# Squares on ScalarE and low-part products last, while float64 weights are converted in a chained attention, MoE and feed-forward kernel

## The chip, the cores and the metric

The kernel runs on one core of one Trainium2 chip. The metric is the device time of one execution in microseconds, as the median of several runs. Five engines of the core work side by side, each through its own list of instructions in order: TensorE (matmul), VectorE, ScalarE, GpSimd, and SyncE, which here starts DMA transfers.

## The reference

A sliding-window attention with sink tokens feeds a top-1 mixture of experts, and that feeds a second, dense feed-forward. The change lies in the last part:

```python
def _moe2_ref(x, w_in, w_out):          # x 1536x512, w_in 512x2048, w_out 2048x512
    h = x @ w_in
    r = np.maximum(h, 0.0)
    g = r * r
    return (g @ w_out).astype(np.float32)
```

The weights w_in and w_out arrive as float64; everything else is float32.

## The kernel before

**Precision.** A float32 operand is split into a high part of type float32r and a low part, the rest. A product of two split operands is then three matmuls: high x high, high x low, low x high. The names end in h and l: gh and gl for the activations, wh and wl (yh and yl, or xh and xl, as tiles) for the weights.

**The converter.** The two float64 weight matrices are read as pairs of 32-bit integers, in 16 pieces of 1 MB, eight of w_in and eight of w_out, and rebuilt as float32 by `piece_stage` (L174 to L189). A piece passes four stages. Stage 0: ScalarE scales the upper words (L180), VectorE shifts the lower words (L181). Stage 1: VectorE joins them in two operations (L183, L184). Stage 2: ScalarE writes the high part (L186). Stage 3: VectorE writes the low part (L188), and the raw tile is free for the transfer of a later piece; there are three such tiles of 1 MB. One call of `tick` (class `Ticks`, L191) finishes the piece that is open and begins the next: old stage 2, new stage 0, old stage 3, new stage 1, in that order on each engine. The list of pieces alternates between w_out and w_in after the first two. Three ticks run within the last expert; `ticks.close()` finishes the open piece, and 13 pieces remain. `ticks.done()` is true once the list is used up and nothing is open.

**The second feed-forward.** The 1536 tokens go in three chunks of 512 (index c), the 2048 hidden features in 16 blocks of 128 (index f), so there are 48 steps (c, f). `run` goes through them by the order written out there:

```python
            stage_a(c, f)      # 12 matmuls: block f of h, transposed, 128 x 512 tokens
            stage_g(c, f)      # ScalarE gh, VectorE gl
            tick()             # one round of the converter, while there is work
            if turn:
                its.pop(0)()   # transposes for the next chunk, at f = 7, 9, 11, 13
            if prev:
                stage_b(*prev) # 12 matmuls of the step before: 4 row blocks x 3 products
            prev = c, f
```

`stage_a` ends with the Relu on ScalarE (L1112, from PSUM to an SBUF tile called xb in the trace) and the square on VectorE (L1113, in place). `stage_g` makes gh from it on ScalarE (L1128) and gl on VectorE (L1130). `stage_b` (L1169) adds g @ w_out for one feature block into four PSUM tiles, one for each block of 128 tokens, and works through them one after the other, each with its three products. TensorE's order is thus a(f), b(f-1), a(f+1), b(f), and so on. With 13 pieces left, tick has work in the first 14 steps (c = 0, f = 0 to 13), and `ticks.done()` is still false when `stage_a` runs in each of these 14. When `stage_b` runs, after the tick, it is false for the blocks f = 0 to 11. A piece of w_out serves two feature blocks.

Of the kernel before, what the change touches and what calls it, by code (L numbers as in the profile page):

```python
# [12 lines left out]
AF = mybir.ActivationFunctionType  # L13
# [3 lines left out]
P = 128  # L17
# [15 lines left out]
def kernel(  # L33
# [15 lines left out]
    nc = tc.nc  # L49
# [8 lines left out]
    NFF = FF // P  # L58
# [27 lines left out]
    def ps(tag, name):  # L86
        banks[tag].append(banks[tag].pop(0))
        return psum.tile([P, 512], F32, tag=f"b{banks[tag][-1]}", name=name)
# [10 lines left out]
    def raw_tile(n=1):  # L99

        nonlocal slot
        slot += slot % n
        t = RAW[slot // 2 % len(RAW)][:, slot % 2 * 1024 : slot % 2 * 1024 + n * 1024]
        slot += n
        return t
# [657 lines left out]
    for u in range(len(units) + PL + 1):  # L763
# [4 lines left out]
        if u < len(units):  # L768
            n, c = units[u]
# [17 lines left out]
        m, c = divmod(u, HP)  # L787
# [196 lines left out]
    ticks = Ticks(order)  # L984
# [17 lines left out]
    def load_y(c, tags):  # L1002

        c0, w = chunks[c]

        def ld(t):
            if t < w // P:
                r0 = c0 + t * P
                nc.sync.dma_start(yts[t % len(yts)], yd[r0 : r0 + P, :])

        def go(t):
            yt = yts[t % len(yts)]
            p_ = ps(tags[t % 2], "x2T")
            for kk in range(KD):
                nc.tensor.transpose(p_[:, kk * P : (kk + 1) * P], yt[:, kk * P : (kk + 1) * P], ident)  # L1015
            n = c0 // P + t
            nc.gpsimd.tensor_copy(tok[:, n : n + 1], yt.bitcast(I32)[:, DM:])
            pv = p_.rearrange("p (k n) -> p k n", k=KD)
            hv, lv = (x[:, :, t * P : (t + 1) * P] for x in x2T[c])
            nc.scalar.copy(hv, pv)  # L1020
            nc.vector.tensor_sub(lv, pv, hv.bitcast(F32))  # L1021
            ld(t + len(yts))

        for t in range(len(yts)):
            ld(t)
        return [lambda t=t: go(t) for t in range(w // P)]
# [70 lines left out]
    outp, gT, its, scattered = {}, {}, [], []  # L1097

    def stage_a(c, f):
        nonlocal its  # L1100
        if f == 0:
            its = load_y(c + 1, ("pt", "ot")) if c + 1 < NCH else []
        a_ = ps("bg", "a")
        xh, xl = x2T[c]
        w = width[c]
        for kk in range(KD):
            r = slice(f % 2 * 512 + kk * P, f % 2 * 512 + kk * P + P)
            wh, wl = WI.h[f // 2][:, r], WI.l[f // 2][:, r]
            for m, (a, bb) in enumerate(((wh, xh), (wh, xl), (wl, xh))):
                nc.tensor.matmul(a_[:, :w], a, bb[:, kk, :w], start=(kk == 0 and m == 0), stop=(kk == KD - 1 and m == 2))  # L1110
        r_ = xring[f % 2, last][:, :w]
        nc.scalar.activation(r_, a_[:, :w], AF.Relu)  # L1112
        nc.vector.tensor_mul(r_, r_, r_)  # L1113
        gT[c, f] = r_


# [4 lines left out]
    def packed(c):  # L1121
        return width[c] % P if 0 < width[c] % P <= 64 else 0
# [12 lines left out]
    def scatter(n, o_, rows):  # L1135
        i = nc.gpsimd.indirect_dma_start(  # L1136
            out=out, out_offset=bass.IndirectOffsetOnAxis(ap=tok[:rows, n : n + 1], axis=0), in_=o_[:rows, :], in_offset=None,
            bounds_check=NTOK - 1, oob_is_err=False,
        )

        for x in scattered:
            tc.declare_no_dep(i.ins, x.ins, reason="rows of different tokens")
        scattered.append(i)

    def blocks(c):

        ts = list(range((width[c] + P - 1) // P))
        return ts[-1:] + ts[:-1] if packed(c) else ts

    def stage_b(c, f, only=None):  # L1150
        gh, gl = gT[c, f]
        w, k_ = width[c], packed(c)
        nt = (w + P - 1) // P
        if f == 0:
            outp[c] = [ps("s" if t < 3 else "iv", "out") for t in range(nt)]
        wh, wl = WO.h[f // 2], WO.l[f // 2]
        r = slice((f % 2) * 512, (f % 2) * 512 + 512)
        for t in blocks(c) if only is None else [only]:
            cs = slice(t * P, min(w, (t + 1) * P))
            rows = cs.stop - cs.start  # L1160
            o = outp[c][t]
            if k_ and t == nt - 1:
                prods = ((gh[:, cs.start : w + k_], wh), (gh[:, cs.start : w + k_], wl))
                o = o[: 2 * k_, :]
            else:
                prods = ((gh[:, cs], wh), (gh[:, cs], wl), (gl[:, cs], wh))
                o = o[:rows, :]
            for m, (a, bb) in enumerate(prods):
                nc.tensor.matmul(o, a, bb[:, r], start=(f == 0 and m == 0), stop=(f == NFF - 1 and m == len(prods) - 1))  # L1169
            if f == NFF - 1:  # L1170
                n = chunks[c][0] // P + t
                o_ = raw_tile()[:, :DM]
                if k_ and t == nt - 1:
                    nc.scalar.copy(o_[:k_, :], o[k_ :, :])
                    nc.vector.tensor_add(o_[:k_, :], o_[:k_, :], o[:k_, :])
                elif t % 2:
                    nc.scalar.copy(o_[:rows, :], o)
                else:
                    nc.vector.tensor_copy(o_[:rows, :], o)
                scatter(n, o_, rows)  # L1180
# [5 lines left out]
    def run(steps, prev):  # L1186

        for c, f in steps:
            turn = f >= 7 and f % 2 and its
            stage_a(c, f)  # L1190
            stage_g(c, f)
            tick()
            if turn:
                its.pop(0)()
            if prev:
                stage_b(*prev)
            prev = c, f
        return prev

    def end(c, prev):  # L1200

        nonlocal slot
        slot = 0
        for f in (NFF - 2, NFF - 1):
            stage_a(c, f)
            stage_g(c, f)
        stage_b(*prev)
        for t in blocks(c):
            stage_b(c, NFF - 2, t)
            stage_b(c, NFF - 1, t)  # L1210
# [60 lines left out]
```

## Time and profile before

| | us |
|---|---|
| median of 3 runs | 607.14 |
| lowest and highest of them | 607.09, 607.84 |
| the profiled execution, its own time | 608.54 |
| span of the profiled execution | 606.8 |
| TensorE busy (share of span) | 575.8 (95%) |
| VectorE busy | 354.9 (58%) |
| ScalarE busy | 297.2 (49%) |
| GpSimd busy | 136.5 (22%) |

The span goes from the first to the last instruction; the profiled execution's own time is longer than that by 1.7 us. Rows of the trace are all from this one execution. Busy shares are averages over parts of the kernel that have different limits. A matmul's shown duration overlaps with the next one's, since they are pipelined: the pace is the distance between starts.

### The profile page before, as it was taken

To read this page: it belongs to the slowest core of one execution; us is meant where nothing else is said; L and a number is where in the kernel's file an instruction comes from. 1 tells how busy PE (TensorE), PEld (TensorE's weight loads), DVE (VectorE), ACT (ScalarE), POOL (GpSimd) and SP (SyncE) were. 2 spreads that over 40 slices of the span, in tenths; PEclk is the share of its full clock that TensorE was granted. 3 is DMA by queue.
4 is the path that set the end of the run, shared out by engine and by line. 5 is a ranking of instruction groups with operands and counts; after the bars stand their busy time and mean duration, and the time that the engine had idled before them with its cause. 6 is when DMAs were issued, how large, how long until landed. Compare 5 with 4: busy or idle time off the path is not lost. (4 is left out here: it accounts for less than half of the span.)

```text
span 606.8 us, 9356 instructions
## 1 busy us (share of the span) xinstructions
PE 575.8 (95%) x3243; PEld 458.7 (76%) x3243; DVE 354.9 (58%) x838; ACT 297.2 (49%) x649; POOL 136.5 (22%) x235
## 2 busy tenths in 40 slices
PE   8999999979999999999899899999999999999994
PEld 4777778758887787777687677777888888888883
DVE  3788888747449966957752798996322322322222
ACT  4788878636248756746532455544222221322221
POOL 8544455233223413422211000000200000200002
PEclk9999999989999999999999899999999999999998
DMA  8698996446527985856731946441100000100001
GB/s 186 166 217 162 213 202 150 139 120 196 173 49 241 346 308 151 298 181 215 241 104 57 357 166 199 157 139 52 59 11 1 17 1 0 59 15 2 0 1 60
DMA packets 74625, 82.09 MB, mean 135 GB/s; under 512 B 42200, under 2 KB 53464, under 8 KB 74560
## 3 DMA queue, kind: packets, MB, share of 16 engines
q1 hardware_dynamic: 70608, 72.45, 41.6%
q0 software_dynamic: 3952, 8.82, 4.2%
q8 instruction: 35, 0.57, 0.4%
q14 instruction: 30, 0.25, 0.1%
HBM read 69.29 MB, written 16.08 MB: 141 GB/s over the span
## 5 line engine op out<-in xcount | busy, mean ns | idle before, releaser
L1113 DVE TENSOR_TENSOR xb<-xb 128x512 f32<-128x512 f32 (+1 forms) x48 | 31.6, 658 | 104.6 <-ACT xb L1112 104.6
L1112 ACT ACTIVATE xb<-a 128x512 f32<-128x512 f32 (+1 forms) x48 | 27.6, 575 | 113.8 <-PE a L1110 113.7
L1169 PE MATMUL out<-yl,gh 128*128 128x512 f32 (+1 forms) x188 | 75.8, 403 | 4.1 <-DVE yl L188 4.1
L1169 PE MATMUL out<-yh,gh 128*128 128x512 f32 (+1 forms) x188 | 75.7, 402 | 1.9 <-ACT gh L1128 1.9
L1169 PE MATMUL out<-yh,gl 128*128 128x512 f32 x173 | 68.8, 398 | 0.0
L1128 ACT CAST gh<-xb 128x512 fp32r<-128x512 f32 (+1 forms) x47 | 28.0, 597 | 64.1 <-DVE xb L1113 60.6
L454 ACT ACTIVATE p<-p,nm 128x260 f32<-128x260 f32 (+2 forms) x96 | 46.9, 489 | 17.3 <-DVE nm L442 16.2
L957 POOL DMA_INDIRECT yd<-ys,dst x14 | 26.0, 1857 | 118.7 <-DVE xl L145 33.3
L1130 DVE TENSOR_TENSOR gl<-xb,gh 128x512 fp32r<-128x512 f32 (+1 forms) x47 | 30.7, 653 | 33.8 <-ACT gh L1128 32.5
L1136 POOL DMA_INDIRECT out_dram<-raw,tok x12 | 11.8, 984 | 169.2 <-issue 69.5
L1110 PE MATMUL a<-x2Al,xh 128*128 128x512 f32 (+1 forms) x128 | 47.9, 374 | 0.6 <-DVEq L1078 0.6
L1110 PE MATMUL a<-x2Ah,xh 128*128 128x512 f32 (+1 forms) x128 | 48.2, 376 | 0.3 <-PEq L1078 0.3
L1110 PE MATMUL a<-x2Ah,xl 128*128 128x512 f32 (+1 forms) x128 | 47.8, 374 | 0.0
L1169 PEld LDWEIGHTS out<-yl,gh 128*128 128x128 f32 (+1 forms) x188 | 34.9, 186 | 14.5 <-DVE yl L188 6.2
L145 DVE TENSOR_TENSOR yl<-raw,yh 128x512 fp32r<-128x512 f32 x64 | 40.4, 686 | 5.8 <-ACT yh L144 5.7
L1169 PEld LDWEIGHTS out<-yh,gh 128*128 128x128 f32 (+1 forms) x188 | 34.8, 185 | 10.9 <-ACT gh L1128 2.4
L1169 PEld LDWEIGHTS out<-yh,gl 128*128 128x128 f32 x173 | 32.9, 190 | 8.1 <-DVE gl L1130 0.4
L144 ACT CAST xh<-raw 128x512 fp32r<-128x512 f32 x64 | 36.2, 619 | 1.1 <-DMA raw<-in_moe_w_dram 0.8
L144 ACT CAST yh<-raw 128x512 fp32r<-128x512 f32 x64 | 35.5, 623 | 2.2 <-PEq L969 1.7
L914 DVE TENSOR_TENSOR hTl<-hT,hTh 128x512 fp32r<-128x512 f32 x28 | 19.3, 690 | 28.4 <-ACT hTh L913 28.4
L145 DVE TENSOR_TENSOR xl<-raw,xh 128x512 fp32r<-128x512 f32 x48 | 30.2, 687 | 1.9 <-ACT xh L144 1.6
L529 PE MATMUL ot<-pts,v 128*64 128x128 f32 x352 | 30.1, 286 | 0.5 <-ACT pts L496 0.5
(224 smaller groups left out, 1407.8 us busy)
## 6 DMA issues: line engine op xcount, KB each, us to landing
raw<-in_moe_w_dram SPq DMA_DIRECT2D x64, 512.0 KB, 4.6
raw<-in_moe_w_in_dram SPq DMA_DIRECT2D x16, 512.0 KB, 4.8
raw<-in_moe_w_out_dram SPq DMA_DIRECT2D x8, 1024.0 KB, 5.3
yd<-zero SPq DMA_DIRECT2D x12, 256.5 KB, 6.3
xd<-x SPq DMA_DIRECT2D x12, 256.5 KB, 5.0
xb<-yd SPq DMA_DIRECT2D x12, 256.5 KB, 4.4
kr<-in_k_dram SPq DMA_DIRECT2D x12, 256.0 KB, 5.7
qr<-in_q_dram SPq DMA_DIRECT2D x12, 256.0 KB, 6.2
```

The lines of the kernel that those rows point to most:

```text
L144: (hi or nc.scalar.copy)(self.h[i][:, sl], t[:, sl])
L145: (eng or nc.vector).tensor_sub(self.l[i][:, sl], t[:, sl], self.h[i].bitcast(F32)[:, sl])
L454: nc.scalar.activation(d["p"][:, h, :width], d["p"][:, h, :width], AF.Exp, bias=d["nm"][:, h : h + 1], scale=-1.0, accum_out=d["sm"][:, h ...
L529: nc.tensor.matmul(d["o"][i * D : (i + 1) * D, c * P : (c + 1) * P], vt[b, kb][:, h, :], t_, start=i not in d["started"], stop=False, skip ...
L914: nc.vector.tensor_sub(l_, p_, h_.bitcast(F32))
L957: nc.gpsimd.indirect_dma_start(out=yd[:, :], out_offset=bass.IndirectOffsetOnAxis(ap=dst[:, b, e : e + 1], axis=0), in_=y_, in_offset=None ...
L1110: nc.tensor.matmul(a_[:, :w], a, bb[:, kk, :w], start=(kk == 0 and m == 0), stop=(kk == KD - 1 and m == 2))
L1112: nc.scalar.activation(r_, a_[:, :w], AF.Relu)
L1113: nc.vector.tensor_mul(r_, r_, r_)
L1128: nc.scalar.copy(gh[:, :w], r_)
L1130: nc.vector.tensor_sub(gl[:, : w - k_], r_[:, : w - k_], gh.bitcast(F32)[:, : w - k_])
L1169: nc.tensor.matmul(o, a, bb[:, r], start=(f == 0 and m == 0), stop=(f == NFF - 1 and m == len(prods) - 1))
```

## The change

While `ticks.done()` is false, the square of `stage_a` becomes an activation with the function Square on ScalarE instead of a multiplication on VectorE. Also while it is false, `stage_b` for the first chunk issues its 12 products in another order: for each of the three products of high and low parts it goes over the four row blocks, with the product of gh and the low part of the weights as the last of the three. After that everything is as before.

```diff
         nc.scalar.activation(r_, a_[:, :w], AF.Relu)
-        nc.vector.tensor_mul(r_, r_, r_)
+
+        if ticks.done():
+            nc.vector.tensor_mul(r_, r_, r_)
+        else:
+            nc.scalar.activation(r_, r_, AF.Square)
         gT[c, f] = r_
...
         r = slice((f % 2) * 512, (f % 2) * 512 + 512)
-        for t in blocks(c) if only is None else [only]:
+        ts = blocks(c) if only is None else [only]
+        if not ticks.done() and c == 0 and f < NFF - 1:
+
+            for a, bb in ((gh, wh), (gl, wh), (gh, wl)):
+                for t in ts:
+                    nc.tensor.matmul(
+                        outp[c][t], a[:, t * P : (t + 1) * P], bb[:, r], start=(f == 0 and a is gh and bb is wh), stop=False
+                    )
+            return
+        for t in ts:
             cs = slice(t * P, min(w, (t + 1) * P))
```

## Rows read from the trace of the kernel before

**Rows 1.** Stretches of the span: busy time and instructions by engine, granted TensorE clock, DMA.

```profile
core 0: us, PE busy (x) PEld busy (x) DVE busy (x) ACT busy (x) POOL busy (x), PEclk, DMA share, GB/s
336.30:340.80 4.50, 4.45 (x12) 3.20 (x13) 4.33 (x5) 1.53 (x2) 0.00 (x0) 0.63 1.09 384
...
343.86:413.00 69.14, 65.10 (x282) 51.08 (x280) 61.21 (x71) 37.72 (x48) 1.50 (x4) 1.00 0.51 169
413.00:529.00 116.00, 115.97 (x507) 93.71 (x508) 37.82 (x56) 30.62 (x52) 7.54 (x11) 1.00 0.07 23
529.00:597.00 68.00, 68.00 (x326) 59.09 (x325) 18.84 (x44) 15.40 (x29) 1.05 (x2) 1.00 0.02 9
```

**Rows 2.** Waits from 330 to 414 us: who for whom, total, times, longest.

```profile
PE out L1169 <- DVE yl L188: 4.1, 6, 0.9
...
PEld out L1169 <- DVE gl L1130: 0.4, 1, 0.4
```

**Rows 3.** Instructions in order of time, 352 to 363 us: start, duration, instruction, idle.

```profile
352.36 0.68 DVE L1113 TENSOR_TENSOR xb<-xb 128x512 f32<-128x512 f32 x1
...
353.08 0.62 ACT L1128 CAST gh<-xb 128x512 fp32r<-128x512 f32 x1 [2.75 <-DVE xb L1113]
...
353.61 1.13 ACT L186 CAST xh<-raw 128x1024 fp32r<-128x1024 f32 x1
...
353.73 0.69 DVE L1130 TENSOR_TENSOR gl<-xb,gh 128x512 fp32r<-128x512 f32 x1 [0.69 <-ACT gh L1128]
...
354.34 0.69 DVE L181 TENSOR_SCALAR raw<-raw 128x1024 int32<-128x1024 int32 x1
...
354.63 1.17 ACT L180 ACTIVATE raw<-raw 128x1024 f32<-128x1024 f32 x1
...
354.94 1.22 DVE L188 TENSOR_TENSOR xl<-raw,xh 128x1024 fp32r<-128x1024 f32 x1
...
355.82 0.60 ACT L1112 ACTIVATE xb<-a 128x512 f32<-128x512 f32 x1
...
356.08 1.22 DVE L183 SCALAR_TENSOR_TENSOR raw<-raw 128x1024 int32<-128x1024 int32 x1
...
357.33 1.23 DVE L184 SCALAR_TENSOR_TENSOR raw<-raw 128x1024 int32<-128x1024 int32 x1
...
358.48 0.69 DVE L1113 TENSOR_TENSOR xb<-xb 128x512 f32<-128x512 f32 x1
...
361.19 0.39 PE L1169 MATMUL out<-yh,gh 128*128 128x512 f32 x1
...
362.33 0.49 PE L1169 MATMUL out<-yl,gh 128*128 128x512 f32 x1 [0.76 <-DVE yl L188]
...
362.66 0.40 PE L1169 MATMUL out<-yh,gl 128*128 128x512 f32 x1
```

**Rows 4.** Chain that ended last, in order of time: start, duration, what.

```profile
415.87 2.81 PE a L1110 x12
418.69 2.80 PE out L1169 x12
...
480.77 0.44 PE x2T L1015 x4
```

**Rows 5.** Groups by form, 330 to 412 us: count, busy us, mean ns, idle before.

```profile
L1128 ACT CAST gh<-xb 128x512 fp32r<-128x512 f32 x13 | 8.1, 620 | 37.6 <-DVE xb L1113 34.1 <-DMA yd<-ys,dst 3.4
L1112 ACT ACTIVATE xb<-a 128x512 f32<-128x512 f32 x13 | 7.8, 601 | 6.7 <-PE a L1110 6.6
...
L1021 DVE TENSOR_TENSOR x2Bl<-x2T,x2Bh 128x512 fp32r<-128x512 f32 x3 | 2.0, 683 | 0.0
```

**Rows 6.** Page section 6, DMA issues: KB each, microseconds from issue to landing.

```profile
raw<-in_moe_w_out_dram SPq DMA_DIRECT2D x8, 1024.0 KB, 5.3
```

**Rows 7.** Instructions in order of time, first step of the second feed-forward.

```profile
335.68 0.62 ACT L1128 CAST gh<-xb 128x512 fp32r<-128x512 f32 x1 [3.44 <-DMA yd<-ys,dst]
```

**Rows 8.** Groups of ScalarE by form, whole span.

```profile
L377 ACT ACT_TABLE_LOAD x1 | 1.3, 1283 | 0.8 <-PEq L1255 0.8
```

## The prediction

> **What bounds the kernel now.** I read the windows first. In the second feed-forward TensorE is busy 115.97 of 116.00 us from 413 to 529 and all 68.00 us from 529 to 597, at a granted clock of 1.00 [rows 1]. These stretches are bound by TensorE alone, and a delay before them reaches the end of the kernel in full. The stretch from 343.86 to 413 is different: 65.10 of 69.14 us busy at the same full clock, so about 4 us of TensorE stood idle, while VectorE was busy for 61.21 us [rows 1]. That is where the float64 weights are converted. The change acts there and nowhere else: 14 steps run while the converter has work.
>
> The waits name what TensorE missed: 4.1 us in six waits for a low part of the output weights (yl, written at L188), the longest 0.9 us [rows 2]. Six fits the code: a piece of w_out serves two steps, so every second stage_b is the first to read a fresh yl.
>
> Why yl is late is seen in one step in order of time [rows 3]. VectorE begins a square at 352.36 and the next at 358.48, a period of 6.12 us. In between it is idle only once, 0.69 us before gl, waiting for ScalarE's gh, and gh itself had waited for the square. So VectorE's own chain sets the period: square and the wait for gh take 353.73 - 352.36 = 1.37 us, and gl, L181, L188, L183, L184 take 358.48 - 353.73 = 4.75 us. TensorE needs less for a step. Twelve products of stage_a take 2.81 us and twelve of stage_b 2.80 us [rows 4], together 5.61 us. VectorE loses 0.51 us per step to it, and TensorE pays once in two steps, at yl.
>
> **What TensorE lost.** A wait costs more than its idle time, since the pipe has to start again. At 361.19 the first product starts, and its third at 362.66, 1.47 us later [rows 3]. At the unhindered pace of 2.80/12 = 0.233 us it would be 0.47 us. The delay is 1.00 us, of which 0.76 is shown as idle [rows 3], so 0.24 us comes on top of each wait. Six waits: 4.1 + 6 x 0.24 = 5.5 us. The periods agree: about eleven steps between the first and the last wait, at 6.12 - 5.61 = 0.51 us each, are 5.6 us.
>
> **The change part by part.** (a) Fourteen squares leave VectorE. With each goes its 0.72 us slot (352.36 to 353.08), and VectorE no longer has to be done with a square before gh can start [rows 3]. If it still had to stand for gh's 0.65 us, its step would be 6.12 - 0.72 = 5.40 us; if not, 4.75 us. Both are under TensorE's 5.61 us.
>
> (b) Fourteen squares come to ScalarE, 128x512 float32 in place in SBUF. The rows have no Square. The nearest are the cast gh, the same size from SBUF, with 620 ns, and the Relu from PSUM with 601 ns [rows 5]; above lies the 1.17 us of L180, twice as wide [rows 3]. Below nothing speaks for less than 0.60. I take 0.62. ScalarE's step then is gh, L186 and L180 (353.08 to 355.80, 2.72 us), Relu 0.60 [rows 3] and Square 0.62: 3.94 us, or 4.5 us at the upper price. It was idle for 2.75 us before gh [rows 3], and that idle time is the cover. It stays under 5.61 us at either price, so I cost it at nothing.
>
> Whether a new function brings table loads with it is seen in the forms of ScalarE: one table load in the whole span, 1,283 ns [rows 8], although Exp, Relu, scaled copies and casts alternate all through. The Trainium skill (ScalarE: Activation LUTs, section "Table sets: the hidden batching unit") speaks against mixing functions: functions are loaded in sets, and each switch to another set costs a load; relu, copy, identity and abs are said to be in every set, and square isn't named there. The single load of this trace agrees for the functions already used and says nothing on Square; that is the second rival.
>
> (c) What follows in the chain. Let stage_a's last product end at T. ScalarE runs Relu, Square and gh one behind the other to about T + 1.9; gl then follows on VectorE. L186 starts 0.53 us after gh starts (353.08 to 353.61) and takes 1.13 [rows 3], to about T + 2.9. VectorE meanwhile does gl and L181, starts L188 at about T + 3.2 and ends it near T + 4.4. The stage_b that reads this yl comes after the other stage_b and the next stage_a, at T + 5.6 [rows 4]. So yl is there 1.2 us early. With Square at 1.17 us it is still 0.6 us early. The next thing late would be VectorE's last conversion L184: it ends about 4.75 us after gl began, T + 6.7, and the next gl can start only at T + 7.5. The transfers keep up: a raw tile comes free when L188 ends and is converted two steps later, some 10 us, against 5.3 us to landing [rows 6].
>
> (d) Four steps (7, 9, 11, 13) also carry transposes of the next chunk, 0.44 us on TensorE [rows 4], and three L1021 of 683 ns on VectorE in this window [rows 5]. VectorE's 4.75 + 0.68 = 5.43 us stays under 5.61.
>
> (e) The new order of the products in steps with f = 0 to 11: gh x wh over the four row blocks, then gl x wh, then gh x wl. The count stays 12. Each product already loads its own weights (507 products, 508 loads from 413 to 529 us [rows 1]), and a change of output block every third product doesn't stretch the 0.233 us pace [rows 4], so changing it at every product should cost nothing (bounds: nothing, and at most one more such pace a step, which no row shows). It puts the first use of wl 8 x 0.233 = 1.9 us later. Once the square is off VectorE, yl is early without this, so it adds little: it is spare room. Its other end is gl, now needed four products into a stage_b instead of two; only the very first stage_b waited for gl, 0.4 us seen at the weight load [rows 2], and that may go, worth 0 to 0.4; I take 0.1.
>
> (f) What isn't moved: the first gh starts at 335.68 after a transfer of the experts' results has released its buffer [rows 7], and the half-speed stage_b behind that (granted clock 0.63, the clock then near its lower level of 1.2 GHz for much of 336.3 to 340.8) [rows 1] comes from the idle time before it. Neither is touched.
>
> The sum: -5.5 - 0.1 = -5.6 us. The profiled execution took 608.54 us with a span of 606.8; it becomes 602.9 with a span of 601.2. The median of the runs is 607.14, 1.4 us under the profiled one, so the forecast is 601.5 us. Since TensorE has no gap left there, more than the whole of 5.5 + 0.4 can't be had: 601.2; with a spread of the runs of 0.75 us the range begins at 600.6.
>
> **The rivals.** First, part of the gain (603.3 us). In the steps with transposes VectorE could still stand for gh: 4.75 + 0.68 + 0.69 = 6.12 us, 0.51 over TensorE's 5.61 in three steps, 1.5 us; a slower pace at changes of output block (0.03 us in a few dozen products) could add a few tenths. So -5.6 + 1.8. For it: ScalarE does L1020's copy in those steps as well. Against it: the transposes lengthen TensorE's step by 0.44 too, and the spare 0.8 us of (c) covers one such step.
>
> Second, slower: Square isn't in the loaded set, and each step switches to it and back. Place: between Relu, Square and gh. Price: two loads of 1.283 us [rows 8], so ScalarE's step is 3.94 + 2.57 = 6.51 us, 0.39 over the present 6.12; over some twelve steps +4.7 us: 611.8 us. It decides from the point where the two loads together pass 6.12 - 3.94 = 2.18 us, 1.09 each. For it: no row shows a Square. Against it: one load served four kinds of operations, and one set that held Square with Relu and copy would cost a single load, hidden. By the page's 2.66 us for a switch with its drain, an estimate would be 645 us.
>
> Third, no change (607.1 us): L188 is held by something other than VectorE's own load, such as the transfers or ScalarE's L186. Against it: VectorE has no idle time before L188 in the step shown, and its one gap is the wait for gh that the change shortens [rows 3].
>
> **How the numbers follow.** Forecast, whole gain: 0.82. Part of it: 0.10. No change: 0.04. Slower: 0.04. A measurement of this kernel can tell about 0.2%, 1.2 us, from no change; the first two cases are faster by more than that, so 0.92 faster, 0.04 same, 0.04 slower. The range runs from 600.6 (all waits gone, lower end of the spread) to 603.6 (the first rival with a little spread); it leaves out the last two cases and tails of the first.
>
> **What would show it.** Right: no wait of TensorE for yl from 340 to 410; ScalarE shows 14 Square of about 0.62 us and still one table load; squares at L1113's old place start at step 14 only; VectorE has idle time before gl in each step of the conversion, about 0.8 us; the gap-free pace of 5.61 us per step starts at about 341 instead of 413, and the span is near 601.2. Wrong: table loads beside the Squares, waits that go over to gh or gl in front of stage_b, a Square well over 1.2 us, or a pace of stage_b above 0.233 us per product.

## The result, and the profile after

| | before | after |
|---|---|---|
| median, us | 607.49 (4 runs, 607.09 to 609.78) | 601.05 (4 runs, 600.77 to 602.40) |
| profiled execution, us | 608.54 | 600.88 |
| its span, us | 606.8 | 599.2 |
| TensorE busy in it, us | 575.8 | 573.0 |

The ratio is 0.9891, 95% interval 0.9868 to 0.9914: 1.1% faster, 6.4 us between the medians. The forecast was 601.5 us, in a range of 600.6 to 603.6.

**The stretches.** The columns of the windows of the changed kernel are those of [rows 1]. The first line here is the first stage_b of the second feed-forward, the second goes from the next stage_b to the stage_a behind the stage_b of f = 12:

```profile
core 0: us, PE busy (x) PEld busy (x) DVE busy (x) ACT busy (x) POOL busy (x), PEclk, DMA share, GB/s
336.19:339.09 2.90, 2.90 (x13) 2.36 (x13) 2.76 (x4) 2.76 (x4) 0.00 (x0) 1.00 1.09 383
341.88:408.11 66.23, 66.23 (x294) 53.44 (x292) 58.29 (x63) 48.84 (x64) 2.12 (x4) 1.00 0.59 194
```

The same two pieces of work in the kernel before:

```profile
336.35:341.06 4.71, 4.71 (x13) 3.41 (x13) 4.33 (x5) 1.69 (x3) 0.00 (x0) 0.64 1.09 383
343.86:415.71 71.85, 67.77 (x293) 53.26 (x292) 63.88 (x73) 37.85 (x48) 1.50 (x4) 1.00 0.52 173
```

In the conversion TensorE is now busy for all of 66.23 us where it had 4.1 of 71.85 us idle: 5.62 us less, and 5.5 was the forecast for it. The other line is a surprise: the first stage_b took 2.90 us at a granted clock of 1.00, before 4.71 us at 0.64, 1.81 us less. These two and a start 0.16 us earlier (336.35, 336.19) make 7.6 us, as the spans do.

**The waits** from 325 to 410 us, which answer to [rows 2] (who for whom, total, times, longest):

```profile
DVE gl L1134 <- ACT gh L1132: 12.3, 10, 6.0
...
PE out L1167 <- ACT gh L1132: 1.6, 1, 1.6
...
DVE raw L181 <- DMA raw<-in_moe_w_out_dram: 0.8, 1, 0.8
```

TensorE waits for the first gh, and no longer for yl. VectorE waits for gh in ten steps, 6.0 us in the first and 0.7 us on average in nine of the 13 that follow: there it has time to spare.

**One step** on ScalarE, answering to [rows 3]:

```profile
358.92 0.60 ACT L1112 ACTIVATE xb<-a 128x512 f32<-128x512 f32 x1 [1.20 <-PE a L1110]
359.55 0.63 ACT L1117 ACTIVATE xb<-xb 128x512 f32<-128x512 f32 x1
360.21 0.62 ACT L1132 CAST gh<-xb 128x512 fp32r<-128x512 f32 x1
360.74 1.14 ACT L186 CAST xh<-raw 128x1024 fp32r<-128x1024 f32 x1
361.77 1.16 ACT L180 ACTIVATE raw<-raw 128x1024 f32<-128x1024 f32 x1
364.51 0.60 ACT L1112 ACTIVATE xb<-a 128x512 f32<-128x512 f32 x1 [1.57 <-PE a L1110]
```

and on VectorE:

```profile
359.09 1.23 DVE L184 SCALAR_TENSOR_TENSOR raw<-raw 128x1024 int32<-128x1024 int32 x1
360.87 0.69 DVE L1134 TENSOR_TENSOR gl<-xb,gh 128x512 fp32r<-128x512 f32 x1 [0.56 <-ACT gh L1132]
361.48 0.69 DVE L181 TENSOR_SCALAR raw<-raw 128x1024 int32<-128x1024 int32 x1
362.08 1.22 DVE L188 TENSOR_TENSOR xl<-raw,xh 128x1024 fp32r<-128x1024 f32 x1
363.22 1.22 DVE L183 SCALAR_TENSOR_TENSOR raw<-raw 128x1024 int32<-128x1024 int32 x1
364.47 1.23 DVE L184 SCALAR_TENSOR_TENSOR raw<-raw 128x1024 int32<-128x1024 int32 x1
```

Relu, Square and gh stand one behind the other on ScalarE. VectorE finishes L184 at 360.32, stands still for 0.56 us and goes on with gl; the step is 358.92 to 364.51 on ScalarE, 5.59 us, TensorE's own 5.6.

**The chain that ended last** is now TensorE's from 336.19 on, where in the kernel before TensorE's whole groups of twelve come in only behind 413 us, as those of [rows 4] (each start here is the end of the product ahead):

```profile
336.19 3.06 PE out L1167 x12
339.25 2.79 PE a L1110 x12
342.04 2.81 PE out L1167 x12
...
405.47 2.81 PE out L1182 x12
408.27 2.81 PE a L1110 x12
```

**The forms of ScalarE** [rows 5, 8]: 14 Square of 633 ns, and still one table load.

```profile
L1117 ACT ACTIVATE xb<-xb 128x512 f32<-128x512 f32 x14 | 8.9, 633 | 0.4
...
L377 ACT ACT_TABLE_LOAD x1 | 1.3, 1283 | 0.8 <-PEq L1268 0.8
```

### The profile page after: what moved, and what is told of

The parts are those of the page before. It is cut to its first block, busy times and chain, and to the rows that moved or that the text cites. A ratio compares the mean times of both kernels' runs of the same rounds, so it can differ in the third digit from the quotient of the medians.

```text
span 599.2 us, 9341 instructions
## 1 busy us (share of the span) xinstructions
PE 573.0 (96%) x3241; PEld 458.5 (77%) x3243; DVE 346.2 (58%) x824; ACT 307.1 (51%) x663; POOL 137.6 (23%) x235
## 5 line engine op out<-in xcount | busy, mean ns | idle before, releaser
L1115 DVE TENSOR_TENSOR xb<-xb 128x512 f32<-128x512 f32 (+1 forms) x34 | 22.0, 648 | 104.3 <-ACT xb L1112 104.3
L1182 PE MATMUL out<-yh,gh 128*128 128x512 f32 (+1 forms) x140 | 55.7, 398 | 0.0
L1182 PE MATMUL out<-yl,gh 128*128 128x512 f32 (+1 forms) x140 | 55.5, 397 | 0.0
L1182 PE MATMUL out<-yh,gl 128*128 128x512 f32 x125 | 49.3, 394 | 0.0
L902 ACT ACTIVATE hs<-h 128x512 f32<-128x512 f32 x28 | 16.7, 598 | 28.9 <-PE h L899 24.8
L1182 PEld LDWEIGHTS out<-yh,gh 128*128 128x128 f32 (+1 forms) x140 | 25.5, 182 | 6.5
L1182 PEld LDWEIGHTS out<-yl,gh 128*128 128x128 f32 (+1 forms) x140 | 25.5, 182 | 6.2
```

## The experiments

Two measures recur. *The stretch* goes from the first product of the second feed-forward to the end of the span in the profiled execution (before: 327.67 to 606.83, 279.16 us; after: 327.82 to 599.17, 271.35 us). It leaves out what the attention and the experts do, where single executions differ by a few us. *VectorE's chain* goes from the start of the first gl to the start of the low part of the sixth later piece of w_out, the yl that the stage_b of f = 12 reads (before: 336.33 to 411.76, 75.43 us; after: 336.17 to 402.63, 66.46 us). The stretch and the chain are read from one execution of each kernel, the medians from all. The first stage_b, and whether it ran at half clock, is named with each, from its first product to the first of the next stage_a. A ratio is to the kernel before on the same chip, whose medians were 608.3 to 608.6 us in the later runs. The ends of VectorE's chain, in the kernel before and in the changed one:

```profile
336.33 0.69 DVE L1130 TENSOR_TENSOR gl<-xb,gh 128x512 fp32r<-128x512 f32 x1 [3.37 <-ACT gh L1128]
...
411.76 1.22 DVE L188 TENSOR_TENSOR yl<-raw,yh 128x1024 fp32r<-128x1024 f32 x1
```

```profile
336.17 0.69 DVE L1134 TENSOR_TENSOR gl<-xb,gh 128x512 fp32r<-128x512 f32 x1 [5.99 <-ACT gh L1132]
...
402.63 1.22 DVE L188 TENSOR_TENSOR yl<-raw,yh 128x1024 fp32r<-128x1024 f32 x1
```

| kernel | stretch, us | first stage_b, us (granted clock) | median, us | ratio to before |
|---|---|---|---|---|
| before | 279.16 | 4.71 (0.64) | | |
| changed | 271.35 | 2.90 (1.00) | 601.05 | 0.9891 (0.9868 to 0.9914) |
| changed, again | 273.46 | 4.45 (0.62) | 600.75 | 0.9868 (0.9847 to 0.989) |
| squares only | 273.39 | 4.71 (half clock) | 602.63 | 0.9923 (0.9894 to 0.9952) |
| order only | 279.18 | 4.32 (half clock) | 608.48 | 1.0005 (0.9989 to 1.0021) |
| Relu twice | 271.46 | 2.90 (full) | 602.94 | 0.9921 (0.9899 to 0.9942) |
| Relu five times | 284.11 | 2.90 (full) | 612.06 | 1.0064 (1.004 to 1.0088) |
| squares moved in steps 0 to 6 | 275.20 | 4.37 (half clock) | 603.20 | 0.9912 (0.9882 to 0.9942) |
| all 48 squares moved | 273.26 | 4.42 (half clock) | 602.69 | 0.99 (0.9874 to 0.9927) |
| changed, other place for first gh | 269.31 | 2.72 (full) | 597.61 | 0.9823 (0.9796 to 0.985) |
| before, other place for first gh | 276.45 | 2.73 (full) | 606.06 | 0.9963 (0.9943 to 0.9984) |
| before, idle time filled | 280.57 | 3.13 (1.00) | 609.18 | 1.002 (0.9989 to 1.005) |

**The squares alone.** The order of the products stays as before.

```diff
-        nc.vector.tensor_mul(r_, r_, r_)
+        if ticks.done():
+            nc.vector.tensor_mul(r_, r_, r_)
+        else:
+            nc.scalar.activation(r_, r_, AF.Square)
```

> The squares of the 14 conversion steps go to ScalarE, the order of the products stays as before. Theory A (VectorE's own chain of 6.12 us a step was the bound, and taking the square out of it is the whole gain; the new order is spare room): no wait of TensorE for yl, 601 to 601.4 us, the time of the full change within 0.4 us. Theory B (the late use of the low weights brings a main share): 603.5 us or more, with waits of TensorE for yl left. Theory C, on the first stage_b alone (in the profile of before it ran at half clock, in that of the change at full clock; by C that is an accident of the single execution and not of the change): the time does not tell, the first stage_b may take 3 or 4.7 us here.

Its waits show none for yl; what is left is in the first stage_b:

```profile
PE out L1173 <- ACT gh L1132: 2.0, 1, 2.0
...
PEld out L1173 <- DVE gl L1134: 0.4, 1, 0.4
```

The stretch, 273.39 us, is that of the full change with a first stage_b at half clock (273.46). The squares are the whole gain of the stretch. The median, 602.63 us, was expected at 601 to 601.4 and lies 1.6 us above that of the changed kernel. Those of two kernels with the squares on ScalarE and the new order (Relu twice, all squares) lie as high, so the order is not what sets these three apart from the changed kernel; what does stays open. Whole times, which hold the attention and the experts too, don't settle what the order is worth here; the stretches, one execution each, do to a few tenths.

**The order alone.**

```diff
-        for t in blocks(c) if only is None else [only]:
+        ts = blocks(c) if only is None else [only]
+        if not ticks.done() and c == 0 and f < NFF - 1:
+            for a, bb in ((gh, wh), (gl, wh), (gh, wl)):
+                for t in ts:
+                    nc.tensor.matmul(
+                        outp[c][t], a[:, t * P : (t + 1) * P], bb[:, r], start=(f == 0 and a is gh and bb is wh), stop=False
+                    )
+            return
+        for t in ts:
```

> The squares stay on VectorE, the products of the 12 steps go in the new order. Theory A: VectorE still needs 6.1 us a step, and the stage_b of f = 12, which has the old order again, needs its yl at the second product, so TensorE's delay is only gathered there: 606.8 to 607.5 us, no gain beyond 0.5 us, one wait for yl of some 4 to 5 us at f = 12 or a few late ones. Theory B: the use 1.9 us later hides the waits: 601 to 604 us.

```profile
PE out L1163 <- ACT yh L186: 2.5, 4, 0.9
...
PE out L1163 <- ACT gh L1128: 2.0, 1, 2.0
...
PE out L1178 <- DVE yl L188: 0.9, 1, 0.9
PE out L1178 <- ACT yh L186: 0.9, 1, 0.9
```

No gain: 1.0005, and a stretch of 279.18 against 279.16 us. VectorE's chain is 75.46 us (339.35 to 414.81), before 75.43. The place of the waits was not as expected. TensorE did not gather all its delay at f = 12; it now ran ahead until it stood at the high part yh (L186), which the same chain makes late, and it stood at both yh and yl where f = 12 has the old order again. Hiding the use of a late result moved the wait to another result of the same chain.

**ScalarE's cover.** In the full change, the Relu of the 14 steps runs twice, or five times, with the same values.

```diff
-        nc.scalar.activation(r_, a_[:, :w], AF.Relu)
+        for _ in range(1 if ticks.done() else 5):
+            nc.scalar.activation(r_, a_[:, :w], AF.Relu)
```

> The full change, and in the 14 steps the Relu runs twice (the same values into the same tile), 0.5 to 0.6 us more on ScalarE per step. Theory A with ScalarE's 4 us under TensorE's 5.61 us: no change against the full change, 601.0 us within 0.4. Rival (ScalarE's time before gh is on the path from step to step): about 0.55 x 12 = 6 us more, 607 us.

> The full change, and in the 14 steps the Relu runs five times, 2.0 to 2.4 us more on ScalarE per step, which makes 6.0 to 6.4 us. Theory A: now ScalarE is over TensorE's 5.61 us by 0.4 to 0.8 us in some 13 steps, less the 1.2 us that yl had to spare: 605 to 610 us. If ScalarE's limit lies elsewhere than at TensorE's step, the time stays at 601.

One more Relu a step costs nothing in the stretch: 271.46 against 271.35 us, and TensorE waits for no gh behind the first. The median, 602.94 us, is 1.5 us over the expected 601.0 within 0.4, as in two other kernels (above), and 4 us under the rival's 607. With five, ScalarE is never idle (in order of time):

```profile
348.98 3.10 ACT L1113 ACTIVATE xb<-a 128x512 f32<-128x512 f32 x5
352.12 0.63 ACT L1118 ACTIVATE xb<-xb 128x512 f32<-128x512 f32 x1
352.78 0.62 ACT L1133 CAST gh<-xb 128x512 fp32r<-128x512 f32 x1
353.31 1.16 ACT L186 CAST xh<-raw 128x1024 fp32r<-128x1024 f32 x1
354.38 1.17 ACT L180 ACTIVATE raw<-raw 128x1024 f32<-128x1024 f32 x1
355.46 3.10 ACT L1113 ACTIVATE xb<-a 128x512 f32<-128x512 f32 x5
```

From one Relu to the next is 355.46 - 348.98 = 6.48 us, more than the 6.0 to 6.4 expected, 0.87 over TensorE's 5.61. Over 13 steps that is 11.3 us, less the 1.2 us to spare 10.1; the stretch is 284.11 - 271.35 = 12.8 us longer, of which 1.55 us are a stage_b that ran at half clock after its waits (4.38 us for eleven products, where 2.83 is the usual after such a wait):

```profile
415.20 4.38 PE out L1183 x11
```

The idle time before the first stage_b is also 0.44 us longer here (2.05 against 1.61); 0.7 us are left unexplained. So the kernel became slower than before by loading ScalarE past TensorE's step: the mechanism is as expected, and the miss above 610 us comes from the larger step and from the half clock, which was not expected there.

**Half of the steps.** Squares on ScalarE only in steps 0 to 6.

```diff
-        if ticks.done():
+        if ticks.done() or (c, f) >= (0, 7):
             nc.vector.tensor_mul(r_, r_, r_)
```

> The full change, but only the squares of f = 0 to 6 go to ScalarE; in the conversion steps 7 to 13 they are on VectorE again. Theory A (VectorE's chain of 6.1 us a step against TensorE's 5.6, with the spare room of yl in between): from gl of step 7 to the end of yl of step 12 VectorE took 34.8 us before; begun at 372.0 as in the profile of the full change it ends at 406.9, 1.2 us after TensorE wants it there: stretch from the first product of the second feed-forward to the end 272.4 to 273.0 us, 1.7 us more if the first stage_b runs at half clock. Rival (each square moved brings its fourteenth of the gain of 7.8 us): 275 us.

```profile
PE out L1182 <- DVE yl L188: 0.9, 1, 0.9
...
PE out L1182 <- ACT yh L186: 0.6, 1, 0.6
```

The stretch is 275.20 us with a first stage_b at half clock. Theory A had 274.1 to 274.7 us for that case, so the time lies 0.5 us above its range, mostly because the full change with a half clock had 273.46 and not 273.1; over that it is 1.74 us, where 1.1 to 1.6 were expected. By its number alone the rival's 275 us fits better. But the rival's 7.8 us hold what the clock and a shorter idle time gave to one execution; at half clock the full gain is 279.16 - 273.46 = 5.70 us, and half of it would leave 276.3 us. What speaks for theory A is the place of the waits: behind the first stage_b there are these two alone, both in the old order of f = 12, while VectorE squares again from step 7 on. So the gain does not go by the number of squares: VectorE may lag for some steps before TensorE notices.

**All squares.**

```diff
-        if ticks.done():
-            nc.vector.tensor_mul(r_, r_, r_)
-        else:
-            nc.scalar.activation(r_, r_, AF.Square)
+        nc.scalar.activation(r_, r_, AF.Square)
```

> All 48 squares go to ScalarE, also in the 34 steps without conversion. Theory A (behind the conversion TensorE alone sets the pace): no change against the full change, 271.35 us within 0.5 for the stretch, at most a few tenths less at the very end. Rival (VectorE matters there too): a gain of more than 0.5 us.

273.26 us with a first stage_b at half clock, against 273.46: no change, as expected. Outside the conversion the square's engine does not matter for the stretch.

**The clock of the first stage_b.** The changed kernel once more:

> The changed kernel once more, for the half clock behind the idle time before the first stage_b. Theory C (whether it comes is an accident of the single execution): this kernel shows stretches of either 271.4 us (first stage_b 3.1 us) or 273.1 us (4.7 us), and its times spread by 1.5 us or more, where the kernel with another place for the first gh, which has no such idle time, spread from 597.5 to 598.3 us. If the change itself kept the clock up: always 271.4 us.

```profile
335.25:339.70 4.45, 4.45 (x13) 3.50 (x13) 4.31 (x6) 3.30 (x5) 0.00 (x0) 0.62 1.09 382
```

This time the same program ran its first stage_b in 4.45 us at 0.62, 1.55 us more, behind 2.20 us of idle time instead of 1.61; the stretch is 2.1 us longer, the sum of both. VectorE's chain is 68.01 us here (335.23 to 403.24), 1.55 us more than the 66.46 above: now it follows TensorE. Of the nine profiles that have the idle time in front of that stage_b (1.61 to 2.20 us), six show the half clock there; the two with the shortest idle time (1.61 and 1.82 us) do not, nor does one with 2.05 us. What decides in a single execution stays open. The times spread over 2.6 us (598.93 to 601.50), as expected.

**The idle time filled**, in the kernel before.

```diff
             stage_a(c, f)
+            if (c, f) == (0, 1):
+                fl = ps("ot", "fl")
+                for _ in range(10):
+                    nc.tensor.matmul(fl, zb[:, :P], zb, start=True, stop=True)
             stage_g(c, f)
```

> The kernel before, with ten matmuls on zeros in TensorE's idle time before the first stage_b. If the half clock there comes from that idle time: granted clock 1.00 in the first stage_b, 3.0 to 3.3 us for it instead of 4.7, and VectorE's chain behind it, which sets the pace, unmoved: the stretch to the end stays within 0.5 us of 279.2 us, because what TensorE gains there it then waits for at yl. If TensorE's half-speed stage_b did reach the end: 277.5 us.

```profile
335.05:338.18 3.13, 3.13 (x14) 2.35 (x13) 2.99 (x4) 1.45 (x2) 0.00 (x0) 1.00 1.09 384
```

The first stage_b ran at full clock in 3.13 us, and VectorE's chain took 75.45 us (335.00 to 410.45) as in the kernel before: what TensorE won there it waited for later, at yh and yl. Behind the first two of these waits its clock fell after all, in the third stage_b:

```profile
347.35 0.49 PE L1169 MATMUL out<-yh,gh 128*128 128x512 f32 x1 [0.60 <-ACT yh L186]
348.78 0.50 PE L1169 MATMUL out<-yl,gh 128*128 128x512 f32 x1 [0.94 <-DVE yl L188]
...
350.09 0.63 PE L1169 MATMUL out<-yh,gh 128*128 128x512 f32 x1
350.51 0.63 PE L1169 MATMUL out<-yl,gh 128*128 128x512 f32 x1
```

From 350.1 to 352.6 us the granted clock was 0.50, a product every 0.43 us instead of 0.23, and VectorE's chain did not change by that either. The stretch is 1.4 us longer than expected because of one pause in the third chunk, behind the branches by which the kernel chooses that chunk's width (416 tokens in these executions), that waits for nothing the profile shows (chain in order of time):

```profile
522.79 1.89 PE a L1110 x10
524.68 1.45 issue
526.12 0.53 PE a L1110 x2
```

Without those 1.45 us it is 279.12 us, the 279.16 of before. So in the kernel before a half clock in the first stage_b, or in the third, cost nothing; VectorE led anyway. In the changed kernel TensorE leads from there, and it costs its full 1.55 us.

**Another place for the first gh and gl**, in the changed kernel and in that before: a weight tile that is written only in step 13.

```diff
         gh, gl = ghl[2 if (c, f) == (NCH - 1, NFF - 1) else f % 2]
+        if (c, f) == (0, 0):
+            gh, gl = WO.h[7][:, :CH], WO.l[7][:, :CH]
```

> The full change, and the first gh and gl lie in a weight tile that nobody uses until step 13, so that they don't wait for the transfer of the experts' results. From the first product of the second feed-forward to the end of the span the full change took 271.35 us, before 279.16 us, of which 1.7 us were a first stage_b at half clock. Theory: the idle 1.6 to 2.0 us of TensorE in front of the first stage_b go, and with them any half clock behind it: 269.3 to 269.9 us for that stretch, and a median 1.5 to 2 us under that of the full change. Rival: the wait only moves on to the second gh or to the weights of the next step: 271 us.

> The kernel before, with the same other place for the first gh and gl. Theory A (VectorE's chain of 6.12 us a step is the bound): what TensorE gains at the first stage_b it must give back in part only, since VectorE's chain starts earlier as well, by about the same 2 us: stretch 275.3 to 275.9 us (277.45 less 1.6 to 2.0). If VectorE's chain started no earlier, 277.4.

Chain of the changed kernel with it:

```profile
327.63 5.65 PE a L1110 x23
333.28 2.72 PE out L1169 x12
336.00 2.80 PE a L1110 x12
```

TensorE goes from the second stage_a into the first stage_b without a pause, at full clock: 269.31 us, 2.0 us less than the changed kernel at its best, and 597.61 us, the fastest of all kernels here, with runs from 597.52 to 598.31. The median is 3.1 to 3.4 us under those of the changed kernel, where 1.5 to 2 were expected against one at full clock; against its execution at half clock the stretch is 4.15 us shorter. In the kernel before, the stretch is 2.7 us shorter, and 0.5 to 1.1 us longer than expected. I had started from 277.45, the stretch without the half clock; since that cost nothing, the start is 279.16, and what counts is how much earlier VectorE's chain begins. The first gl came 8.66 us after the first product (327.67 to 336.33), here 5.98 us (327.85 to 333.83): 2.68 us, and the stretch is 2.71 us shorter. The chain itself is 75.51 us long, at a granted clock of 1.00 throughout.

## Why the prediction was right

**What bounded the kernel**: as predicted. VectorE's chain was 75.4 to 75.5 us in each of four kernels that square on VectorE, whatever TensorE's clock, order or start; with the squares gone it is 66.46 or 68.01 us and follows TensorE.

**The gain in the conversion**: 5.5 us forecast, 5.62 us measured between the same two products.

**The Square**: 0.62 us forecast, 633 ns measured. From start to start it is 0.63 us from Relu to Square and 0.66 from Square to gh, where each reads what the one ahead writes, and 0.53 from gh to L186, which does not read gh. ScalarE's cover held, and with five Relu it was shown where it ends. The second rival fell: one table load. The Trainium skill (ScalarE: Activation LUTs, "Table sets: the hidden batching unit") warns of switches between sets; here one load of 1,283 ns served Exp, Relu, copies and Square.

**The chain after** (c): gl began 1.95 us after Relu's start in the step shown (358.92 to 360.87), forecast T + 1.9. VectorE's idle time, forecast 0.8 us in each step, is 0.7 in nine steps; four of the first have none. One point of (c) was off: transfers were to have 10 us. In the first steps VectorE has work left to catch up with and runs a step in 4.9 us, and L181 waited 0.8 us for a transfer once. TensorE didn't notice.

**The order** (e): forecast worth nothing but 0.1 us; alone it brought 0.0, and with and without it the stretches are 273.46 and 273.39. A few tenths either way are not excluded.

**The term that was mis-sized** is (f), "Neither is touched". The prediction counted as lost what TensorE visibly waited in the conversion, in one execution whose first stage_b ran at half clock, and left that stage_b as it was. But its loss was hidden behind VectorE before and is not hidden after, so the gain hangs on whether the clock falls: 5.70 us of the stretch where the changed kernel has the half clock too (279.16 less 273.46), near the forecast 5.6, and 7.81 us where it hasn't. The bound of 5.5 + 0.4 us did not hold.

That the time came out within 0.5 to 0.8 us of 601.5 is in part luck. The medians gained 6.4 us in the first series and 7.75 in the later one (608.50 to 600.75), 0.8 to 2.2 more than the forecast 5.6; but the sum started from 607.14 us, 0.4 to 1.5 us under the later medians of the kernel before, and the two misses offset each other. How many executions had the half clock isn't known, since only a profile shows where it falls.

Two steps of the working don't add up as written; neither carries the forecast. 601.2 less 0.75 is 600.45 and not 600.6, and six waits two steps apart span ten steps, not eleven (5.1 us instead of 5.6). The first rival, part of the gain, did not occur: no step with transposes shows a wait of TensorE.

## What to carry to other kernels

Where a stretch is bound by a chain on one engine, the gain of shortening it runs until the next engine is bound, and that engine's own delays, hidden until then, become part of the time: look for them (idle starts, half clock) before pricing the change, and take them as the next thing to mend. Measure the chain from its first to its last instruction over several kernels; if it keeps its length while everything around it changes, it is the bound. Using a late result later doesn't help when the chain that makes it sets the pace.

## What the runs showed of the hardware

TensorE's granted clock fell to its half level (1.2 of 2.4 GHz) in the first stage_b in six of the nine profiles that have idle time in front of it, behind 1.93 to 2.20 us of it; behind 1.61, 1.82 and, once, 2.05 us it did not. That stage_b then took 4.3 to 4.7 us instead of 2.90. With ten matmuls on zeros in the gap, or with no gap, the clock was full there in all three kernels that had them. Two shorter waits close together were followed by the half level as well: 0.60 and 0.94 us in the kernel with the gap filled, 1.40 and 0.93 us with five Relu. The kernel before has waits of up to 0.9 us without it.
